# Every batch's attention in float32, with q, k and v laid out by the host: a fused attention and MoE kernel on one core

## The chip, the cores and the metric

The kernel runs on one core of one Trainium2 chip. The metric is the device time of one execution in microseconds (us); the number compared is the median of the timed runs. The engines are named as in the profile: PE (TensorE matmuls), PEld (TensorE weight loads), DVE (VectorE), ACT (ScalarE), POOL (GpSimd) and SP (SyncE, which here only issues DMA transfers).

## The reference

Three stages follow each other. The attention part, cut to what matters, is this (4 batches, 8 heads, 576 positions, 64 numbers a head):

```python
q_d, k_d, v_d = mean of every 4 rows of q, k, v         # 144 rows
out_d = softmax(q_d @ k_d.T / 8) @ v_d                  # pooled attention
out_up = repeat each row of out_d 4 times               # 576 rows again
scores = where(|i - j| < 4, q @ k.T / 8, -1e9)          # a band of 7
x = out_up + softmax(scores) @ v
...
xn = x / rms(x) * rms_g                                 # MoE1, x is 2304 x 512
x = ((silu(xn @ w_gate) * (xn @ w_val)) @ w_out)
y = (s * relu(x @ w_in) ** 2 + b) @ w_out2              # MoE2
```

The weights of both MoE stages are float64 in memory.

## The kernel before, in words

**The matmuls of MoE1 and MoE2.** A weight is read as pairs of 32-bit words, made float32 by two ACT and two DVE instructions a piece (L662 to L668), and split into a high and a low float16 half. Each product is three float16 matmuls (high·high, high·low, low·high). MoE1 goes over 8 blocks of 288 tokens. In a block, `moe1_gv` makes 12 pairs of `pg` and `pvl` (12 matmuls each, L746), then ACT takes a tanh (L753), DVE makes `u` in two instructions (L754, and `mul` at L210), and ACT and POOL split it (L757, L758). `moe1_out` makes four `po` of 36 matmuls (L768). The accumulators `pg`, `pvl` and `po` share one ring of PSUM tiles, so a new `pg` waits until DVE has read an older one.

**Attention.** A unit is a pair of heads, with four units to a batch. The local band is done in 9 windows of 64 queries against 70 keys, in two groups of 5 and 4 windows (`JS`). The pooled part has 144 queries in 3 pieces.

- Batches 0 and 1 (`early_unit`) use float32 on TensorE. q and k come in rows of 64 numbers (`load_unit`, L255), and TensorE turns them, 12 transposes (L463) and 4 copies on ACT (L465) a unit. POOL adds up groups of four columns (L468, L469). Scores `sl` (L482) start with a matmul that adds the mask (L478), the pooled scores are `sd` (L500), probabilities are turned (`tpl` L492, `tpd` L517) and multiplied with v (`pvd` L384, `pl` L400).
- Batches 2 and 3 (`attn_unit`) use float16 halves: ACT takes sums of squares for a scale (`stats`), ACT and DVE split q and k (L546, L547), SP turns them by DMA (L550), DVE copies q into blocks (`q_b` L554, `qd_b` L569), TensorE pools (`pd` L562), DVE and ACT split the probabilities (L575, L576, L584, L585), SP turns these too (L578, L588), and POOL and ACT split v (L150 to L152, into `vh` and `vdh`).

**What sets the order.** Attention of batch 0 runs first, with the preparation of the first weights beside it. Then `main01` makes MoE1 blocks 0 and 1. At every yield of it (a tick; mostly 12 matmuls) the generators of the side work take a step each: batch 1 from its start, batch 2 from tick START2 = 54. Blocks 2 to 5 (`middle`) carry batch 3 from START3 on. A unit starts every UNIT_STEP = 14 ticks in batches 2 and 3 and every 4 in batch 1, and `lag(n)` lets n ticks pass. From tick ORDERED = 50 on PE runs in the order in which the code is written (`tc.manual_schedule`); elsewhere and on the other engines a scheduler orders by priority. MoE2 follows MoE1. `warm` (L429) puts matmuls of no result into batch 0 that keep TensorE busy.

Of the kernel before, what the change touches and what calls it, by code (L numbers as in the profile page):

```python
# [32 lines left out]
NJ = 9  # L33
# [3 lines left out]
FLOATS = 4  # L37
HALF0 = 20
HALF_STEP = 12
# [3 lines left out]
LAG_SS = 3  # L43
LAG_PD = 6
LAG_SD = 3
LAG_SL = 2
LAG_VH = 3
LAG_V = 6
LAG_OD = 2
# [14 lines left out]
PDPE = 2  # L64
DEP = False
AMPB = 3
MASKB = 1
# [5 lines left out]
OFF = 0  # L73
OFF1 = 0
# [15 lines left out]
def kernel(  # L90
    ctx: ExitStack,
    tc: tile.TileContext,
    q: bass.AP,
    k: bass.AP,
    v: bass.AP,
# [37 lines left out]
    accs = [cp.tile([128, 2], F32, name=f"accs{i}") for i in range(2)]  # L133
# [8 lines left out]
    QB = (dve, dve)  # L142
    DEM = pool if DEP else dve
# [35 lines left out]
    def setup():  # L179
# [43 lines left out]
    P_d = ap.tile([128, 12, 128], F16, name="P_d")  # L223
    P_l = ap.tile([128, 18, 128], F16, name="P_l")
    q_b = ap.tile([128, 18, 2, 64], F16, name="q_b")
    qd_b = ap.tile([128, 2, 3, 128], F16, name="qd_b")

    def early_set(places):
        return {k: t[:, o:o + n] if t is not None else ap.tile([128, 2 * n], F16, tag=k, name=k + "0").bitcast(F32)
                for (k, n), (t, o) in zip((("qkT", 1152), ("PlT", 1152), ("vh", 1152), ("PdT", 768)), places)}  # L230

    def flat(t, pat):
        return t.rearrange(pat).bitcast(F32)

    def second_set():

        return early_set([(flat(P_l, "p a b -> p (a b)"), 0), (flat(q_b, "p j h q -> p (j h q)"), 0),
                          (ap.tile([128, 24 * 128], F16, tag="qk", name="qk0").bitcast(F32), 0),
                          (flat(P_d, "p a b -> p (a b)"), 0)])
# [20 lines left out]

    def load_windows(b, hp, vw):
        h0 = 2 * hp
        sp.dma_start(out=vw[:, :, 0, :], in_=v[b, h0:h0 + 2, 0:WIN, :].rearrange("h p d -> p h d"))
        sp.dma_start(out=vw[:, :, 8, :], in_=v[b, h0:h0 + 2, S - WIN:S, :].rearrange("h p d -> p h d"))
        for h in range(2):
            base = v[b, h0 + h, 61:62, 0:1]
            sp.dma_start(out=vw[:, h, 1:8, :],
                         in_=bass.AP(tensor=base.tensor, offset=base.offset, ap=[[D, WIN], [64 * D, 7], [1, D]]))
# [8 lines left out]
    def stats(hp, qkf, vd, junk):  # L277

        acc = accs[hp % 2]
        act.activation(out=junk[:, :1536], in_=qkf.rearrange("p t c h d -> p (t c h d)"), func=AF.Square,  # L280
                       accum_out=acc[:GR, 0:1])
        act.activation(out=junk[:72, :1024], in_=vd.rearrange("p a r d -> p (a r d)"), func=AF.Square,
                       accum_out=acc[:72, 1:2])
        accb = ap.tile([128, 2], BF16, tag="accb", name="accb")
        pool.tensor_single_scalar(out=accb, in_=acc, scalar=TINY, op=ALU.add)
        vs = sum4(vd)
        yield from lag(LAG_SS)
        ss = pX.tile([128, 2], F32, tag="x", name="ss")
        pe.matmul(out=ss, lhsT=ones_b, rhs=accb, start=True, stop=True)
        sc, iv = pow2(ap, ss, 2, 13, "sq", 2)  # L290
        cs = ap.tile([128, 2], F32, tag="cs", name="cs", bufs=2)
        mul(cs[:, 0:1], iv[:, 0:1], 1.0 / 8, iv[:, 0:1])
        dve.tensor_single_scalar(out=cs[:, 1:2], in_=iv[:, 1:2], scalar=2.0 ** -14, op=ALU.mult)
        return vs, sc, cs

    def softmax_d(sd, scale, de=None):
        dm = ap.tile([128, 3], F32, tag="dm", name="dm", bufs=2)
        dz = ap.tile([128, 3], F32, tag="dz", name="dz", bufs=2)
        dve.tensor_reduce(out=dm, in_=sd, axis=AX.X, op=ALU.max)
        dve.tensor_scalar(out=dm, in0=dm, scalar1=scale, scalar2=-1.0, op0=ALU.mult, op1=ALU.mult)  # L300
        if de is None:
            de = ap.tile([128, 3, SD], F32, tag="de", name="de")
# [10 lines left out]
    def scores_d(qd, cs):  # L313
        sd = pX.tile([128, 3, SD], F32, tag="x", name="sd")
        for o in range(3):
            for n, (lq, lk) in enumerate(((0, 0), (0, 1), (1, 0))):
                pe.matmul(out=sd[:, o, :], lhsT=qd_b[:, lq, o], rhs=qd[:, lk, SD:2 * SD], start=n == 0, stop=n == 2)
        de, dz = softmax_d(sd, cs[:, 0:1])
        dve.tensor_scalar(out=dz, in0=dz, scalar1=1e-9, scalar2=2.0 ** -12, op0=ALU.add, op1=ALU.mult)
        dve.reciprocal(out=dz, in_=dz)  # L320
        return de, dz

    def scores_l(qT, kT, js, mask_pe):

        m = len(js)
        sl = pS.tile([128, 5, WIN], F32, tag="s", name="sl")
        if mask_pe:
            pe.matmul(out=sl[:, :m, :], lhsT=ident_b, rhs=mask[:, js[0]:js[0] + m, :], start=True, stop=False,
                      skip_group_check=True)
        for j in js:  # L330
            for i, (lq, lk) in enumerate(((0, 0), (0, 1), (1, 0))):
                pe.matmul(out=sl[:, j - js[0], :], lhsT=qT[lq][:, j].rearrange("p h q -> p (h q)"),
# [825 lines left out]
```

## Time and profile before

| | |
|---|---|
| three timed runs | 1058.77, 1060.12, 1063.67 us; median 1060.12 us |
| profiled execution, span | 1059.3 us |
| PE busy | 976.0 us (92%) |
| DVE, ACT, POOL busy | 595.9, 518.1, 326.1 us |
| DMA packets | 128111, of which 111376 under 512 B |

The span runs from the first to the last instruction of the profiled execution; the runs' median lies 0.8 us above it. An engine's busy time is the union of its instructions. What PE does not fill of the span is waiting; part of its busy time can be at a lower granted clock.

### The profile page before, as it was taken

To read this page: it belongs to the slowest core of one execution; us is meant where nothing else is said; L and a number is where in the kernel's file an instruction comes from. 1 tells how busy PE (TensorE), PEld (TensorE's weight loads), DVE (VectorE), ACT (ScalarE), POOL (GpSimd) and SP (SyncE) were. 2 spreads that over 40 slices of the span, in tenths; PEclk is the share of its full clock that TensorE was granted. 3 is DMA by queue.
4 is the path that set the end of the run, shared out by engine and by line. 5 is a ranking of instruction groups with operands and counts; after the bars stand their busy time and mean duration, and the time that the engine had idled before them with its cause. 6 is when DMAs were issued, how large, how long until landed. Compare 5 with 4: busy or idle time off the path is not lost.

```text
span 1059.3 us, 20473 instructions
## 1 busy us (share of the span) xinstructions
PE 976.0 (92%) x8197; PEld 661.2 (62%) x8198; DVE 595.9 (56%) x1271; ACT 518.1 (49%) x1182; POOL 326.1 (31%) x417
## 2 busy tenths in 40 slices
PE   7985989998879799878999998999999999999998
PEld 4763767876658578756786676754555545455553
DVE  4788976725786645768627867474432414133240
ACT  3876687745546436544537877662322404132140
POOL 7443763354355455445451216320000000000000
PEclk9986999999999899998999999999999999999999
DMA  9884244102444323454204424200000000000000
GB/s 186 228 235 142 75 134 127 37 12 58 95 89 84 68 36 73 86 100 86 38 2 140 144 76 143 97 1 20 11 11 20 1 31 1 20 11 11 20 1 30
DMA packets 128111, 73.59 MB, mean 69 GB/s; under 512 B 111376, under 2 KB 115984, under 8 KB 128016
## 3 DMA queue, kind: packets, MB, share of 16 engines
q1 hardware_dynamic: 128016, 72.29, 26.8%
q8 instruction: 64, 1.05, 0.4%
q14 instruction: 31, 0.25, 0.1%
HBM read 54.97 MB, written 4.72 MB: 56 GB/s over the span
## 4 chain that ended last, share of the span: by engine, by line
PE 41%; DMA 5%; DVE 4%; ACT 3%; issue 1%; POOL 0%; SPq 0%; POOLq 0%; DVEq 0%; ACTq 0%
PE y L1120 18%; PE ph L1100 17%; DMA stg<-in_moe_w_in_dram 2%; PE pvl L746 2%; DMA stg<-in_moe_w_out_dram 2%; PE pg L746 2%; PE po L768 1%; DVE W L668 1%; DVE stg L664 1%; ACT stg L663 1%; ACT W L662 1%; DMA qkT<-qk 0%; DVE W L148 0%; DMA vw<-in_v_dram 0%; ACT W L147 0%
## 5 line engine op out<-in xcount | busy, mean ns | idle before, releaser
L746 PEld LDWEIGHTS <-W 128*128 128x128 f16 x2304 | 225.8, 100 | 99.9 <-issue 39.0
L1100 PE MATMUL ph<-X,W 128*128 128x384 f16 x1152 | 196.6, 326 | 0.4 <-DVE s4o L711 0.3
L746 PE MATMUL pg<-X,W 128*128 128x288 f16 x1152 | 167.7, 294 | 22.0 <-DVE u L754 20.8
L746 PE MATMUL pvl<-X,W 128*128 128x288 f16 x1152 | 164.9, 291 | 9.6 <-DVE u L754 4.9
L1100 PEld LDWEIGHTS <-W 128*128 128x128 f16 x1152 | 112.6, 98 | 81.2 <-issue 1.2
L1120 PE MATMUL y<-W 128*128 128x512 f16 x648 | 151.6, 379 | 0.0
L768 PE MATMUL po<-g,W 128*128 128x288 f16 x1008 | 132.4, 290 | 5.1 <-DVE u L754 4.3
L768 PEld LDWEIGHTS <-W 128*128 128x128 f16 x1152 | 112.9, 100 | 37.2 <-issue 7.4
L1104 ACT ACTIVATE r<-ph 128x384 f32<-128x384 f32 x96 | 46.9, 489 | 175.8 <-PE ph L1100 126.3
L758 POOL TENSOR_TENSOR g<-u,g 128x288 f16<-128x288 f32 x84 | 72.9, 868 | 133.4 <-ACT g L757 132.9
L1120 PEld LDWEIGHTS <-W 128*128 128x128 f16 x648 | 63.4, 98 | 71.0
L210 DVE SCALAR_TENSOR_TENSOR r<-ph,r 128x384 f32<-128x384 f32 x96 | 53.5, 557 | 59.1 <-ACT r L1104 59.1
L1125 DVE SCALAR_TENSOR_TENSOR ys<-y,ccol,bcol 128x512 f32<-128x512 f32 x18 | 13.5, 751 | 121.4 <-PE y L1120 119.2
L757 ACT ACTIVATE g<-u 128x288 f16<-128x288 f32 x84 | 36.8, 438 | 62.8 <-DVE u L210 61.1
L1108 DVE TENSOR_TENSOR W<-r,W 128x384 f16<-128x384 f32 x72 | 40.1, 557 | 36.6 <-ACT W L1107 36.6
L754 DVE SCALAR_TENSOR_TENSOR u<-u,pvl 128x288 f32<-128x288 f32 x96 | 43.0, 448 | 28.7 <-PE pvl L746 20.7
L1107 ACT ACTIVATE W<-r 128x384 f16<-128x384 f32 x72 | 37.5, 521 | 40.0 <-DVE r L210 40.0
L664 DVE SCALAR_TENSOR_TENSOR stg<-stg 128x512 int32<-128x512 int32 (+1 forms) x53 | 36.6, 690 | 33.7 <-ACT stg L663 33.6
L753 ACT ACTIVATE u<-pg,tsc 128x288 f32<-128x288 f32 x96 | 46.7, 487 | 9.4 <-PE pg L746 9.2
L1120 PE MATMUL y<-W,r2b 128*128 128x512 f16 x216 | 50.1, 379 | 0.0
L662 ACT ACTIVATE W<-stg 128x512 f32<-128x512 f32 (+1 forms) x53 | 34.1, 646 | 24.0 <-DMA stg<-in_moe_w_in_dram 10.7
L210 DVE SCALAR_TENSOR_TENSOR u<-u,pg 128x288 f32<-128x288 f32 x96 | 43.1, 449 | 1.6
(266 smaller groups left out, 1410.7 us busy)
## 6 DMA issues: line engine op xcount, KB each, us to landing
stg<-in_moe_w_out_dram SPq DMA_DIRECT2D x25, 512.0 KB
stg<-in_moe_w_in_dram SPq DMA_DIRECT2D x16, 512.0 KB
out_dram<-ys SPq DMA_DIRECT2D x18, 256.0 KB
W<-in_moe_w_gate_dram SPq DMA_DIRECT2D x10, 384.0 KB
W<-in_moe_w_val_dram SPq DMA_DIRECT2D x10, 384.0 KB
qkf<-in_q_dram SPq DMA_DIRECT2D x26, 144.0 KB
qkf<-in_k_dram SPq DMA_DIRECT2D x26, 144.0 KB
vd<-in_v_dram SPq DMA_DIRECT2D x13, 288.0 KB
```

The source lines that it names most:

```text
L210: (eng or dve).scalar_tensor_tensor(out=o, in0=a, scalar=s, in1=b, op0=ALU.mult, op1=ALU.mult)
L662: act.activation(out=dst, in_=stg[:, :, 1].bitcast(F32), func=AF.Copy, scale=2.0 ** -112)
L664: ins = dve.scalar_tensor_tensor(out=stg[:, :, 0], in0=stg[:, :, 1], scalar=-2 ** 31, in1=stg[:, :, 0], op0=ALU.bitwise_and, op1=ALU.bitwi ...
L746: pe.matmul(out=acc, lhsT=Cgv.half(o, FP, lw)[:, f0 * 128:f0 * 128 + 128], rhs=X16[:, kc, 3 * blk:3 * blk + 3, lx, :], start=i == 0, stop= ...
L753: act.activation(out=u, in_=ps[0], func=AF.Tanh, scale=tsc[:, part:part + 1])
L754: dve.scalar_tensor_tensor(out=u, in0=u, scalar=1.0, in1=ps[1], op0=ALU.add, op1=ALU.mult)
L758: pool.tensor_tensor(out=lo, in0=u, in1=hi, op=ALU.subtract)
L768: pe.matmul(out=acc, lhsT=Co.half(fc * 512, 512, lw)[:, m * 128:(m + 1) * 128], rhs=g16(fc)[:, lx, :], start=i == 0, stop=i == 35)
L1100: pe.matmul(out=acc, lhsT=C2.half((p * KC + kc) * 512, 512, lw)[:, f0 * 128:f0 * 128 + 128], rhs=X16[:, kc, 4 * blk:4 * blk + 4, lx, :], s ...
L1104: act.activation(out=r, in_=acc, func=AF.Relu, scale=2.0 ** -23)
L1108: dve.tensor_tensor(out=dst[:, 1, :], in0=r, in1=dst[:, 0, :], op=ALU.subtract)
L1120: pe.matmul(out=y, lhsT=src[:, lx, tt * 128:(tt + 1) * 128], rhs=C3.half(fc * 512, 512, lw), start=i == 0, stop=i == 47)
```

## The change

The host now lays out three arrays: `qk`, head dimension first, with two heads' q and k side by side (128 rows of 1152 numbers for a unit); `vwin`, v in the 9 windows of 70 rows; and `vgrp`, v in the 72 row groups of 8 rows that the pooled part reads. A unit has three loads. `attn_unit`, `stats`, `scores_d`, `scores_l` and `split_v` are gone; one `unit` serves all batches, in float32, without transposes of q and k. In it the multiply of the pooled probabilities is on DVE, the multiplies of the local ones are on POOL as before, and probabilities are turned 4 and 1 to a PSUM tile in place of 3 and 2. After batch 0, two units at a time have buffers of their own. Values of batch 2 are held until `main01` has ended. New lags: 3 ticks from the loads to the first scores, 3 from the last softmax to the first turn, 2 before the values.

```diff
-LAG_SS = 3
-LAG_PD = 6
-LAG_SD = 3
-LAG_SL = 2
-LAG_VH = 3
-LAG_V = 6
-LAG_OD = 2
+LAG_IN = 3
+LAG_SD = 1
+LAG_T = 3
+LAG_TD = 1
+LAG_V = 2
+LAG_O = 2
...
-    def load_unit(b, hp, qkf, vd, vw):
-        h0 = 2 * hp
-        for t, src in enumerate((q, k)):
-            for h in range(2):
-                sp.dma_start(out=qkf[:, t, :, h, :], in_=src[b, h0 + h].rearrange("(c p) d -> p c d", p=GR))
-        sp.dma_start(out=vd.rearrange("p a r d -> p a (r d)"),
-                     in_=v[b, h0:h0 + 2].rearrange("h (t p r) d -> p (h t) (r d)", p=72, r=4))
-        if vw is not None:
-            load_windows(b, hp, vw)
+    def load_unit(b, hp, st, vd):
+        sp.dma_start(out=st["qkT"], in_=qk[b, hp])
+        sp.dma_start(out=vd.rearrange("p a r d -> p (a r d)"), in_=vgrp[b, hp])
+        sp.dma_start(out=st["vw"][:WIN], in_=vwin[b, hp])
...
-    def early_unit(b, hp, sq_sum):
+    def unit(b, hp, sq_sum):
+
+        far = b >= 1
         if b == 0:
-            qkf, vd, vw = staged[hp]
-            st = early[hp]
+            vd, st = staged[hp]
             qd = Xf[:, hp, S + 1152:S + 1440]
         else:
-            st = second_set() if hp % 2 else early_set([(None, 0)] * 4)
-            qkf = ap.tile([GR, 2, 6, 2, D], F32, tag="qkf", name="qkf")
+            st = own_set()
             vd = ap.tile([72, 4, 4, D], F32, tag="vd", name="vd")
...
-                for i in range(3):
-                    pe.transpose(out=tp[:, i, :], in_=qkf[:, t, 3 * g + i].rearrange("p h d -> p (h d)"),
-                                 identity=ident_f[:GR, :GR])
-                act.activation(out=qT[:, 3 * g:3 * g + 3, :], in_=tp, func=AF.Copy)
...
         sl = local(JS[0])
+        if b == 0:
+            yield
+        a0 = softmax_l(sl, JS[0], pool)
+        if far:
+            yield
+        sl1 = local(JS[1])
+        if far:
+            yield from lag(LAG_SD)
         sd = pX.tile([128, 3, SD], F32, tag="x", name="sd")
...
+        dve.tensor_tensor(out=de, in0=de, in1=dz.unsqueeze(2).to_broadcast([128, 3, SD]), op=ALU.mult)
+        a1 = p1.tile([128, TB], F32, tag="u", name="a1", bufs=3)[:, :280].rearrange("p (j k) -> p j k", j=4) if b == 0 else None
+        a1 = softmax_l(sl1, JS[1], dve if b == 0 and hp == NP - 1 else pool, a1)
...
+        yield from lag(LAG_T if far else 1)
+        turn(a0, JS[0])
+        yield from lag(LAG_TD if far else 1)
...
-    def attn_unit(b, hp, sq_sum):
-        mp = b <= MASKB
...
-        for t in range(2):
-            act.activation(out=qv[:, t, 0], in_=qkv[:, t], func=AF.Copy, scale=sc[:GR, 0:1])
-            dve.scalar_tensor_tensor(out=qv[:, t, 1], in0=qkv[:, t], scalar=sc[:GR, 0:1], in1=qv[:, t, 0],
-                                     op0=ALU.mult, op1=ALU.subtract)
-        qkT = ap.tile([128, 24, GR], F16, tag="qkT", name="qkT")
-        sp.dma_start_transpose(out=qkT, in_=qk.rearrange("p a b -> p (a b)"))
...
+        turn(a1, JS[1])
+        if far:
+            yield from lag(LAG_V)
+        od = values_d(vs, PdT, b)
+        yield from lag(LAG_O if far else 1)
+        while b == 2 and not ended:
+            yield
+        for hh in range(2):
+            values_l(b, hp, JS[hh], vw, PlT, od)
```

On SP, at the head of the program, these rows of the kernel before are the first unit's loads and the start of the second's with the first piece of a weight (`W_86` is the space of the weights, in which q, k and the row groups are staged; `vh_111` takes the windows of v).

```order
L255 DMA W_86<-in_q_dram 96x6x64 x2
L255 DMA W_86<-in_k_dram 96x6x64 x2
L256 DMA W_86<-in_v_dram 72x4x256
L263 DMA vh_111<-in_v_dram 70x2x64
L264 DMA vh_111<-in_v_dram 70x2x64
L267 DMA vh_111<-in_v_dram 70x7x64 x2
L255 DMA W_86<-in_q_dram 96x6x64
L659 DMA W_86<-in_moe_w_gate_dram 128x768
```

In the changed kernel the same place of SP's queue reads as follows (`X` and `gx` lend space to the second and third unit).

```order
L216 DMA qkT<-in_qk_dram 128x1152
L217 DMA W_82<-in_vgrp_dram 72x1024
L218 DMA vw<-in_vwin_dram 70x1152
L478 DMA W_82<-in_moe_w_gate_dram 128x768
L216 DMA X<-in_qk_dram 128x1152
L217 DMA W_82<-in_vgrp_dram 72x1024
L218 DMA X<-in_vwin_dram 70x1152
L216 DMA gx<-in_qk_dram 128x1152
```

Ten DMAs stood ahead of the first weight, nine of them the first unit's; now three do, and the bytes of a unit's loads are nearly the same (128 x 1152, 72 x 1024 and 70 x 1152 numbers of four bytes).

On DVE, in a batch 3 unit of the kernel before, these rows stand in the order in which they run; the last one belongs to a MoE1 block.

```order
L547 SCALAR_TENSOR_TENSOR qk<-qkf,sqs,qk 96x768 x2
L585 TENSOR_TENSOR P_l<-ch,P_l 128x5x70
L585 TENSOR_TENSOR P_l<-ch,P_l 128x4x70
L554 COPY q_b<-qkT 64x18x64 x2
L754 SCALAR_TENSOR_TENSOR u<-u,pvl 128x288
L210 SCALAR_TENSOR_TENSOR u<-u,pg 128x288
```

In the changed kernel a batch 3 unit has this on DVE, from the last part of its local softmax to the pooled one (`L573` and `L185` are the two instructions on `u`).

```order
L573 SCALAR_TENSOR_TENSOR u<-u,pvl 128x288
L265 TENSOR_REDUCE z<-ch 128x4
L185 SCALAR_TENSOR_TENSOR u<-u,pg 128x288
L230 TENSOR_REDUCE dm<-sd 128x3
L266 TENSOR_SCALAR z<-z 128x4
L231 TENSOR_SCALAR dm<-dm 128x3
L267 RECIPROCAL z<-z 128x4
L392 TENSOR_SCALAR dz<-dz 128x3
L393 RECIPROCAL dz<-dz 128x3
L394 TENSOR_TENSOR de<-de,dz 128x432
L573 SCALAR_TENSOR_TENSOR u<-u,pvl 128x288
```

The two splits and the copies of q that stood ahead of `u` are gone, as are all other rows of the split; the multiply of `de` is new there, and what stands ahead of a `u` is now softmax work that waits for scores and for ACT's exponentials.

## Rows read from the trace of the kernel before

**Rows 1.** The page's head and its first part: span, busy time by engine.
```profile
span 1059.3 us, 20473 instructions
...
PE 976.0 (92%) x8197; PEld 661.2 (62%) x8198; DVE 595.9 (56%) x1271; ACT 518.1 (49%) x1182; POOL 326.1 (31%) x417
```

**Rows 2.** Busy time by stretch: stretch, length, engines, granted clock, DMA share, GB/s.
```profile
0.00:94.00 94.00, 71.18 (x792) 50.99 (x793) 69.86 (x161) 59.13 (x155) 46.70 (x74) 0.87 0.82 203
94.00:250.00 156.00, 145.43 (x1413) 112.75 (x1412) 108.82 (x244) 103.05 (x254) 79.89 (x101) 0.94 0.30 84
...
250.00:538.00 288.00, 252.50 (x2924) 198.39 (x2925) 190.41 (x450) 146.63 (x346) 138.22 (x157) 0.96 0.36 71
...
555.00:680.00 125.00, 114.90 (x901) 87.85 (x900) 87.45 (x164) 92.68 (x198) 44.42 (x41) 1.00 0.38 127
680.00:1059.30 379.30, 375.03 (x2020) 197.42 (x2017) 135.51 (x246) 110.72 (x217) 8.74 (x28) 1.00 0.04 13
```

**Rows 3.** Timeline of PE, the first projection matmul of MoE1.
```profile
93.95 0.40 PE L746 MATMUL pg<-X,W 128*128 128x288 f16 x1 [1.09 <-ACT X L632]
```

**Rows 4.** Timeline of DVE at the start: start, duration, instruction, idle before it.
```profile
13.62 0.56 DVE L664 SCALAR_TENSOR_TENSOR W<-W 128x384 int32<-128x384 int32 x1 [8.35 <-ACT W L663]
...
16.90 0.52 DVE L357 TENSOR_REDUCE z<-sl 128x5 f32<-128x350 f32 x1 [1.30 <-PE sl L482]
```

**Rows 5.** DMA traffic of the first 50 us.
```profile
DMA packets 20638, 10.37 MB, mean 207 GB/s; under 512 B 17662, under 2 KB 19102, under 8 KB 20632
```

**Rows 6.** Busy time in one late stretch of the start, columns as in rows 2.
```profile
80.00:90.00 10.00, 2.86 (x24) 2.08 (x23) 10.00 (x25) 6.71 (x15) 3.81 (x5) 0.50 0.61 158
```

**Rows 7.** PE's waits from 250 to 538 us: total, times, longest.
```profile
PE pg L746 <- DVE u L754: 15.9, 10, 3.2
PE pl L400 <- DVE poi L206: 5.9, 1, 5.9
PE pvl L746 <- DVE u L754: 4.9, 1, 4.9
PE po L768 <- DVE u L754: 3.5, 1, 3.5
```

**Rows 8.** Timeline of DVE from 488 us on.
```profile
488.48 2.73 DVE L547 SCALAR_TENSOR_TENSOR qk<-qkf,sqs,qk 96x768 f16<-96x768 f32 x2
491.13 3.04 DVE L585 TENSOR_TENSOR P_l<-ch,P_l 128x350 f16<-128x350 f32 x2
496.14 0.92 DVE L554 COPY q_b<-qkT 64x1152 f16<-64x1152 f16 x2 [1.97 <-DMA qkT<-qk]
```

**Rows 9.** Timelines of POOL and of PE at the same place.
```profile
490.36 3.51 POOL L152 TENSOR_TENSOR vh<-vw,vh 70x1152 f16<-70x1152 f32 x1
...
497.60 3.04 PE L746 MATMUL pvl<-X,W 128*128 128x288 f16 x12 [4.86 <-DVE u L754]
```

**Rows 10.** Timeline of PE: one accumulator's 12 matmuls, in batch 1's stretch.
```profile
203.23 1.63 PE L746 MATMUL pg<-X,W 128*128 128x288 f16 x12
204.70 0.29 PE L746 MATMUL pvl<-X,W 128*128 128x288 f16 x1
```

**Rows 11.** Groups of DVE from 238 to 538 us: busy, mean ns, idle before.
```profile
L547 DVE SCALAR_TENSOR_TENSOR qk<-qkf,sqs,qk 96x768 f16<-96x768 f32 x16 | 22.1, 1412 | 0.7 <-ACT qk L546 0.7
...
L585 DVE TENSOR_TENSOR P_l<-ch,P_l 128x280 f16<-128x280 f32 x8 | 10.1, 1258 | 2.2 <-ACT P_l L584 2.2
```

**Rows 12.** Line L746 alone over one float32 and one float16 unit: length, PE, PEld, clock.
```profile
164.25:190.63 26.38, 19.61 (x150) 14.07 (x148) 1.00 0.37 101
279.84:295.76 15.92, 12.79 (x99) 9.01 (x98) 1.00 0.54 107
```

**Rows 13.** All work from 164.25 to 190.63 us, columns as in rows 2; PE's transposes in it.
```profile
164.25:190.63 26.38, 26.38 (x290) 21.34 (x288) 16.19 (x43) 16.64 (x44) 11.27 (x15) 1.00 0.37 101
...
L463 PE MATMUL tp<-ident_f,qkf 96*128 96x96 f32 x12 | 1.5, 245 | 0.0
```

**Rows 14.** Timeline of PE: six pooled-score matmuls in float32 (12 records).
```profile
183.84 0.95 PE L500 MATMUL sd<-X 64*64 64x144 f32 x12
```

More of the change, by code (lines that the diff above doesn't have):

```diff
@@ L221, with own_set, lent_set @@
     ap = attn_cm.__enter__()
[L223 to L239, printed above, removed]
+    SET = (("qkT", 1152), ("PlT", 1152), ("vw", 1152), ("PdT", 768))
+    def own_set():
+        return {k: ap.tile([128, n], F32, tag=k, name=k, bufs=2) for k, n in SET}
+    def lent_set(places):
+        return {k: t[:, o:o + n] for (k, n), (t, o) in zip(SET, places)}
     gx = p1.tile([128, 3456], F32, tag="g16", name="gx")
@@ L275, in sum4 @@
         return vs
[L277 to L294, printed above, removed]
     def softmax_d(sd, scale, de=None):
@@ L301, in softmax_d @@
         if de is None:
-            de = ap.tile([128, 3, SD], F32, tag="de", name="de")
+            de = ap.tile([128, 3, SD], F32, tag="de", name="de", bufs=2)
         for o in range(3):
@@ L311, in lag @@
             yield
[L313 to L332, printed above, removed]
-                          rhs=kT[lk][:, win0(j):win0(j) + WIN], start=i == 0 and not mask_pe, stop=i == 2,
-                          skip_group_check=True)
-        return sl
     last = []
     normed = set()
+    ended = []
     gates = {}
@@ L346, in queued, with softmax_l @@
             yield
-    def softmax_l(sl, js, scale, zs, mask_pe, eng, a=None):
+    def softmax_l(sl, js, eng, a=None):
         m = len(js)
@@ L487, in turn @@
         def turn(a, js):
-            for j0 in range(js[0], js[0] + len(js), 3):
-                m = min(3, js[-1] + 1 - j0)
-                tp = turned(b, 128, "tpl")
+            for j0 in range(js[0], js[0] + len(js), 4):
+                m = min(4, js[-1] + 1 - j0)
+                tp = turned(b, m, "tpl")
                 for i in range(m):
@@ L518, in early_unit @@
             act.activation(out=PdT[:72, 3 * g:3 * g + 3, :], in_=tp[:72], func=AF.Copy)
-        a = p1.tile([128, TB], F32, tag="u", name="a1", bufs=3)[:, :280].rearrange("p (j k) -> p j k", j=4) if b == 0 else None
-        a = softmax_l(sl, JS[1], 1.0 / 8, 1.0, 1, dve if b == 0 and hp == NP - 1 else pool, a)
-        if b == 0 and hp % 2:
-            gates[1 + hp // 2] = tuple(last)
         yield
-        od = values_d(vs.unsqueeze(1), PdT, 0.25, ((0, 0),), b)
-        turn(a, JS[1])
-        yield
@@ L826, in attn_batch @@
         while gens or live:
-            if gens and n >= starts[NP - len(gens)]:
-                if b and NP - len(gens) == floats:
-                    clear()
+            if gens and n >= step * (NP - len(gens)):
                 live.append(gens.pop(0))
@@ L841, in attn_batch @@
         yield from later_norm(b, 1, sq_sum) if b else norm(b, 1, sq_sum)
-    def attn_later(b):
-        sq_sum = ap.tile([128, S], F32, tag="sqsum", name="sqsum")
-        if b == EARLY and FLOATS == NP:
-            clear()
-        gens = [attn_unit(b, hp, sq_sum) for hp in range(NP)]
-        live = []
-        n = halves_ = 0
-        while gens or live:
-            if gens and n % UNIT_STEP == 0:
-                live.append(gens.pop(0))
-            for g in list(live):
-                got = next(g, 0)
-                if got == 0:
-                    live.remove(g)
-                elif got == "half":
-                    halves_ += 1
-                    if halves_ == NP:
-                        live.append(later_norm(b, 0, sq_sum))
-            n += 1
-            yield
-        yield from later_norm(b, 1, sq_sum)
     def later_norm(b, hh, sq_sum):
@@ L1143 @@
     arrays, args = {}, []
-    for name in _INS:
-        a = _np.ascontiguousarray(inputs[name])
+    laid = dict(inputs)
+    heads = (B, NP, 2, S, D)
+    turned = [_np.asarray(inputs[n]).reshape(heads).transpose(0, 1, 2, 4, 3).reshape(B, NP, 128, S) for n in "qk"]
+    laid["qk"] = _np.concatenate(turned, axis=3)
+    v = _np.asarray(inputs["v"]).reshape(heads)
+    rows = _np.array([[win0(j) + i for i in range(WIN)] for j in range(NJ)])
+    laid["vwin"] = v[:, :, :, rows].transpose(0, 1, 4, 2, 3, 5).reshape(B, NP, WIN, 2 * NJ * D)
+    laid["vgrp"] = v.reshape(B, NP, 2, 2, 72, 4, D).transpose(0, 1, 4, 2, 3, 5, 6).reshape(B, NP, 72, 16 * D)
+    for name in ["qk", "vwin", "vgrp"] + _INS:
+        a = _np.ascontiguousarray(laid[name])
         if a.dtype == _np.float64:
```

232 lines of the change are left out of this document (51 added, 181 removed).

## The prediction

> **What bounds the kernel now.** I read the page's head first: PE is busy 976.0 of 1059.3 us [rows 1], so little can be won beyond PE's 83 us of waiting, apart from work that PE sheds. The busy time by stretch [rows 2] says where the waiting lies. From 680 us on PE works 375.0 of 379.3 us in MoE2, which the change does not touch. The rest falls on four stretches: the start, up to the first projection matmul at 93.95 us [rows 3], with 22.8 us without PE; batch 1's stretch (94 to 250 us) with 10.6; batches 2 and 3 (250 to 538 us) with 35.5; and 555 to 680 us with 10.1.
>
> In the start PE is no limit. Its work is attention and filler, and VectorE is busy 69.9 of 94 us, all of 80 to 90 us [rows 2, 6]. VectorE comes to its first softmax only at 16.90 us [rows 4].
>
> From 250 to 538 us the waits of PE name one thing: 24.3 us in 12 waits of `pg`, `pvl` and `po` are for `u` on DVE, and one of 5.9 us is for a small DVE step of a MoE1 block [rows 7]. Why `u` is late is seen at 488 us: VectorE splits q and k (2.73 us for two), then probabilities (3.04 us for two), then waits 1.97 us for the q that a DMA turns, and copies it; `u` stands behind all four [rows 8]. GpSimd splits v for 3.51 us in the same time. PE waits 4.86 us, and its next 12 matmuls take 3.04 us as the row counts them [rows 9], against 1.63 undisturbed [rows 10]: after the wait the clock is granted at the lower of its two levels, 1.2 GHz, for a while.
>
> **The change part by part.** The sum is made against the profiled execution, 1059.3 us of span, and 0.8 us is added for the runs' median, 1060.1.
>
> *Start, -8 us.* A unit's three loads hold 1.2 MB as its nine did, but 17662 of the first 50 us' 20638 packets were under 512 B, at 207 GB/s [rows 5]. The first scores now need only `qk`, 0.59 MB. At that same rate this saves 0.6 MB, 3 us. The first unit's 12 transposes go as well, 1.5 us of PE [rows 13], and their four copies with the waits in between; estimate another 3 us. So the first softmax begins about 6 us earlier. Behind it VectorE has 69.9 less 3 us of work in 77 us, some 10 us of gaps; earlier loads of the other units close a fifth of them, 2 us. VectorE's own work stays (weights are converted as before, softmax is the same), which is why I don't take more. Bounds: 3 us (the bytes alone) and 15 (nearly every gap closed).
>
> *Batch 1, -4 us.* Four units lose their transposes, 1.5 us each [rows 13]: 6 us of PE if PE is the limit throughout, which at 145.4 of 156 us it nearly is. Bounds 2 and 6; I take 4, since some of it falls into waits.
>
> *Batches 2 and 3, -15.5 us,* of four terms:
> - The waits, 35.5 us [rows 2], go if VectorE and GpSimd are relieved. VectorE loses two groups of 22.1 and 10.1 us [rows 11], the other half of the second split, the splits of the pooled probabilities, the copies of q and the scale's steps; it gains a multiply of `de` a unit, about as long as a softmax step of 0.5 us [rows 4]. GpSimd loses the 3.5 us split of v and more, and gains the sums of q and k. What stood ahead of `u` in one piece, 8.7 us at 488 us [rows 8], becomes softmax steps of some 0.5 us each. I take all 35.5 back; what returns is the last term.
> - The lower clock: 0.96 granted over 288 us costs at most 0.04 x 288 = 11.5 us. Nothing is lost where the clock was low while PE waited anyway. Bounds 0 and 11.5; I take 7, nearer to the upper, since the matmuls behind the wait in [rows 9] did run slow.
> - Float32 costs PE more. In batch 1 one float32 unit spans 26.38 us, with PE never idle [rows 13]; 150 of its matmuls are MoE1's [rows 12], at 0.1225 us each (1.47 us for 12, from start to start [rows 10]), 18.4 us. 8.0 are left to attention, 6.5 without the transposes. A float16 unit takes 15.92 - 99 x 0.1225 = 3.8 us [rows 12]. 2.7 us more for 8 units is +22 us. The upper bound counts the transposes as free: 4.2 x 8 = 34.
> - New waits, +5 us. PE's order is fixed, so it stops where scores wait for the `qk` load, issued 3 ticks (4.4 us) ahead, 2.8 us of which are bytes at 207 GB/s; and where a turn waits for softmax, VectorE and ScalarE by turns, and GpSimd's multiply. Behind a stopped turn stand the projections of MoE1, and behind those `u`. The nearest row is the float32 unit of batch 1, with no wait at all [rows 13]; the farthest is the 35.5 us of now. I take 5, near the first.
>
> *555 to 680 us, -3 us.* Batch 3 ends earlier, so its memory is free earlier, and conversions of MoE2's first weight move a block forward, ahead of the 10.1 us of waits here [rows 2]. Bounds 0 and 6.
>
> Sum: 1060.1 - 8 - 4 - 35.5 - 7 + 22 + 5 - 3 = 1029.6, so 1030 us.
>
> **The rivals.**
> - *The start gains nothing.* VectorE is its limit: in [rows 6] it never pauses, and if the earlier softmax only moves gaps behind, the first projection stays at 94 us. For it speaks that VectorE also converts weights there (from 13.62 us on [rows 4]), whose loads the change leaves alone; against it that 10 us of gaps lie after the first softmax. 1038 us, chance 0.10.
> - *Half of the waits stay.* `u` stays late, because softmax steps and `u` still share VectorE and come in bunches, with two units alive at a time. 0.5 x 42.5 = 21, in place of the 5 taken: 1046 us. Against it: a float32 unit in batch 1 leaves VectorE 10 of 26 us free [rows 13]. Chance 0.09.
> - *Float32 is dearer than batch 1 shows.* If the transposes filled holes that the scores would leave, each unit costs 8.0 us as before: +34 in place of +22, 1042 us. Chance 0.05. The Trainium skill has a rule of this direction (FP8 and Floating Point Precision, section TensorE Precision Notes): true float32 goes through the array in four passes. By it the six pooled-score matmuls, 144 columns each, would take 6 x 144 x 4 columns, 1.44 us at 2.4 GHz as an estimate; this case's trace disagrees, 0.95 us in two records each [rows 14]. By the rule a unit would be near 8.5 us (estimate) and the time about 1045 us.
> - *Slower: the turns stop PE.* The turn of the first windows follows the scores by about five accumulators, 7.4 us [rows 10]. Where a softmax chain is longer than that, because its steps queue behind `u` on VectorE or behind the split of g on GpSimd, PE stops once per unit, the projections start late, and the clock falls as in [rows 9]. At the size of today's waits and clock loss (42.5 us) this gives 1067 us. It decides from 5.1 us a unit on (41 us over 8 units lifts 1024.6 to 1065.4). Against it speaks [rows 13], where the same chain under the same projections makes no wait. Chance 0.05.
>
> **How the numbers follow.** The forecast, with gains in all four places, has 0.71; the rivals have 0.10, 0.09, 0.05 and 0.05. 1030 is its time, not a mean. If the better bounds of the start (15) and of the clock (11.5) come together with no new wait, 1013; I leave 0.08 below that. Above 1047 lie the last rival and the upper part of the second, 0.1. Range 1013 to 1047. A measurement of this kernel tells about 0.5%, 5.3 us, from no change: faster is below 1054.8, which every case but the last gives unless two join, 0.91; same 0.05; slower (above 1065.4) 0.04.
>
> **What would show it right or wrong.** In the changed kernel's profile the first softmax on DVE should stand near 11 us and the first `pg` near 86 us. PE's waits for `u` in the stretch of batches 2 and 3 should fall to a few us, and the granted clock there rise towards 1.00. One float32 unit should take PE 6.5 us beside the projections. From the first matmul of MoE2 on nothing should change. The forecast is wrong if new rows stand among PE's waits: `sl` for a `qk` load, `tpl` or `tpd` for POOL's multiply or DVE's `de`, each over 2 us and once a unit; or if `pg` stays at 94 us with VectorE full from 11 us on.

## The result, and the profile after

The changed kernel runs in 1036.88 us (median; 1034.98 to 1037.72) against 1061.11 us for the kernel before on the same chip. The ratio is 0.9771, with a 95% interval of 0.9751 to 0.9791. The profiled executions are 1034.3 and 1059.3 us long, 25.0 us apart; single executions differ from medians by a few us, so totals below are ratios and stretches are profile times.

The page's head of the changed kernel answers to [rows 1]: VectorE, ScalarE and GpSimd lost 85, 57 and 53 us of work, PE only 3.7.

```profile
span 1034.3 us, 19239 instructions
...
PE 972.3 (94%) x7862; PEld 658.5 (64%) x7870; DVE 510.5 (49%) x1095; ACT 461.6 (45%) x1070; POOL 272.9 (26%) x383
```

Cut at four events that PE's timeline of either kernel shows, the 25 us lie as follows (us; block 2 is the first behind `main01`, with batch 1's tokens; block 6 is the first behind all attention):

| from, to | before | changed | difference | forecast |
|---|---|---|---|---|
| start, first `pg` | 93.95 | 93.31 | -0.6 | -8 |
| first `pg`, `pg` of block 2 | 171.87 | 171.00 | -0.9 | -4 |
| `pg` of block 2, of block 6 | 290.02 | 264.43 | -25.6 | -15.5 |
| `pg` of block 6, first `ph` of MoE2 | 123.86 | 125.93 | +2.1 | -3 |
| MoE2 | 379.6 | 379.6 | 0 | 0 |

So the total came out near the forecast, 1030, with three of its four terms missed and one exceeded. That is luck in part: the start and the last stretch fell short by 12.5 us, the two in the middle made up 7 of them, and the first rival's 1038 lies nearer. The two middle terms were forecast for stretches that part at 250 us and not at block 2, so they are best taken together: -19.5 forecast, -26.5 measured. Busy time from block 2 to 6 in the kernel before (columns as in [rows 2]) is this:

```profile
265.82:555.84 290.02, 257.17 (x2949) 202.62 (x2948) 188.10 (x441) 143.37 (x337) 140.07 (x167) 0.96 0.35 69
```

And in the changed kernel, the start, that stretch, and the blocks ahead of MoE2:

```profile
0.00:94.00 94.00, 64.16 (x708) 44.58 (x714) 71.30 (x164) 51.63 (x131) 45.13 (x69) 0.79 0.71 209
...
264.31:528.74 264.43, 264.27 (x2677) 210.04 (x2677) 106.67 (x278) 112.78 (x285) 93.46 (x139) 1.00 0.12 36
...
530.00:655.00 125.00, 112.68 (x882) 87.00 (x882) 80.79 (x152) 83.56 (x182) 39.57 (x40) 0.97 0.34 102
```

PE's idle time from block 2 to 6 fell from 32.9 to 0.2 us, and the granted clock reads 1.00, its upper level. PE's busy time grew by 7.1 us all the same, since float32 costs more.

In the start, VectorE began softmax 4.9 us earlier than in [rows 4], and the first projection did not follow. VectorE's timeline shows the first softmax step and the end of the start (`L483` converts a weight, `L131` splits one, the `L295` at 85.18 is the last attention step of batch 0, `L430` the norm's first step):

```profile
11.57 0.56 DVE L483 SCALAR_TENSOR_TENSOR W<-W 128x384 int32<-128x384 int32 x1 [6.47 <-ACT W L482]
12.05 0.52 DVE L262 TENSOR_REDUCE z<-sl 128x5 f32<-128x350 f32 x1
...
79.63 5.63 DVE L131 SCALAR_TENSOR_TENSOR W<-W,rs 128x384 f16<-128x384 f32 x6
85.18 0.41 DVE L295 TENSOR_TENSOR X<-pl,od 128x256 f32<-128x256 f32 x1
85.52 3.25 DVE L131 SCALAR_TENSOR_TENSOR W<-W,rs 128x384 f16<-128x384 f32 x5
88.69 0.14 DVE L430 TENSOR_SCALAR ms<-ssn 96x3 f32<-96x3 f32 x1
```

PE's timeline has the first scores, the wait for what comes of the norm, and the row that answers to [rows 3]:

```profile
7.65 1.37 PE L360 MATMUL sl<-qkT 64*64 64x70 f32 x20
...
90.43 0.26 PE L442 MATMUL rb<-ident_b,rp 96*128 96x96 bf16 x1 [5.35 <-POOL rp L435]
...
93.31 0.40 PE L565 MATMUL pg<-X,W 128*128 128x288 f16 x1 [1.09 <-ACT X L451]
```

The timeline puts the 5.35 us on GpSimd, but GpSimd works from `ms`, and `ms` at 88.69 us stood behind five splits on VectorE, and these behind six more.

### The profile page after: what moved, and what is told of

Read it like the earlier page. It is cut to its first block, busy times and chain, and to the rows that moved or that the text cites. A ratio compares the mean times of both kernels' runs of the same rounds, so it can differ in the third digit from the quotient of the medians.

```text
span 1034.3 us, 19239 instructions
## 1 busy us (share of the span) xinstructions
PE 972.3 (94%) x7862; PEld 658.5 (64%) x7870; DVE 510.5 (49%) x1095; ACT 461.6 (45%) x1070; POOL 272.9 (26%) x383
## 4 chain that ended last, share of the span: by engine, by line
PE 68%; DVE 11%; DMA 10%; ACT 6%; issue 3%; POOL 1%; SPq 0%; ACTq 0%; DVEq 0%
PE y L904 18%; PE ph L884 18%; PE po L587 10%; PE pvl L565 7%; PE pg L565 7%; DMA stg<-in_moe_w_in_dram 3%; DMA stg<-in_moe_w_out_dram 3%; DVE W L131 2%; DMA W<-in_moe_w_val_dram 2%; DVE W L487 2%; ACT stg L482 1%; ACT W L481 1%; DVE stg L483 1%; DMA stg<-in_moe_w_gate_dram 1%; PE pl L291 1%
## 5 line engine op out<-in xcount | busy, mean ns | idle before, releaser
L565 PE MATMUL pg<-X,W 128*128 128x288 f16 x1152 | 163.1, 289 | 7.3 <-DVE u L573 4.4
L577 POOL TENSOR_TENSOR g<-u,g 128x288 f16<-128x288 f32 x84 | 67.1, 798 | 165.1 <-ACT g L576 145.7
L185 DVE SCALAR_TENSOR_TENSOR r<-ph,r 128x384 f32<-128x384 f32 x96 | 53.5, 557 | 59.4 <-ACT r L888 59.4
L573 DVE SCALAR_TENSOR_TENSOR u<-u,pvl 128x288 f32<-128x288 f32 x96 | 43.1, 449 | 79.0 <-PE pvl L565 75.8
L483 DVE SCALAR_TENSOR_TENSOR stg<-stg 128x512 int32<-128x512 int32 (+1 forms) x53 | 40.1, 757 | 39.9 <-ACT stg L482 39.7
L185 DVE SCALAR_TENSOR_TENSOR u<-u,pg 128x288 f32<-128x288 f32 x96 | 43.2, 449 | 2.0
```

Source lines behind the costliest of these rows:

```text
L185: (eng or dve).scalar_tensor_tensor(out=o, in0=a, scalar=s, in1=b, op0=ALU.mult, op1=ALU.mult)
L483: ins = dve.scalar_tensor_tensor(out=stg[:, :, 0], in0=stg[:, :, 1], scalar=-2 ** 31, in1=stg[:, :, 0], op0=ALU.bitwise_and, op1=ALU.bitwi ...
L565: pe.matmul(out=acc, lhsT=Cgv.half(o, FP, lw)[:, f0 * 128:f0 * 128 + 128], rhs=X16[:, kc, 3 * blk:3 * blk + 3, lx, :], start=i == 0, stop= ...
L573: dve.scalar_tensor_tensor(out=u, in0=u, scalar=1.0, in1=ps[1], op0=ALU.add, op1=ALU.mult)
L577: pool.tensor_tensor(out=lo, in0=u, in1=hi, op=ALU.subtract)
```

## The experiments

Theory A, after the result: the end of the start is set by what VectorE has queued, conversions and splits; batches 2 and 3 gained because VectorE and GpSimd were relieved, and PE is their only bound now; the missing rest went into new waits at 231 and 533 us. The rivals stand with each run. Theories C and D came after the first run. Ratios are to the kernel before on the same chip, with 95% intervals; the changed kernel's is 0.9771, and 0.001 is about 1 us.

**1. The rows alone.** Three loads a unit as in the change, but in short rows:

```diff
-        sp.dma_start(out=st["qkT"], in_=qk[b, hp])
+        sp.dma_start(out=st["qkT"].rearrange("p (c x) -> p c x", c=18), in_=qk[b, hp].rearrange("c p x -> p c x"))
...
+    for n_, c_ in (("qk", 18), ("vwin", 18), ("vgrp", 4)):
+        w_ = laid[n_]
+        laid[n_] = w_.reshape(w_.shape[:3] + (c_, w_.shape[3] // c_)).transpose(0, 1, 3, 2, 4)
```

> The changed kernel, with the same three loads a unit, but laid out in memory so that q, k and the windows of v come in rows of 256 bytes and the row groups in rows of 1 KB. Theory A (the start is set by VectorE's conversions and splits, and no load ends last later on): within 3 us of the changed kernel's 1036.9, first projection matmul at 93 us plus or minus 1. Rival (large rows do pay, 3 us in the start and more where loads are awaited): 5 us or more slower, with PE waits for qkT in batches 1 to 3.

Measured: 0.9723 (0.9697 to 0.9750), 1028.02 us, some 5 us *faster* than the changed kernel, which neither theory had. The first `pg` is at 83.71 us. In PE's timeline:

```profile
83.71 0.40 PE L565 MATMUL pg<-X,W 128*128 128x288 f16 x1 [4.82 <-ACT X L451]
```

And in the DMA traffic of the first 50 us, where most packets are short again, as in [rows 5]:

```profile
DMA packets 24125, 10.87 MB, mean 217 GB/s; under 512 B 21328, under 2 KB 22768, under 8 KB 24118
```

This was no comparison of rows alone, as the order of VectorE's instructions tells: the scheduler had ordered the start anew. Counted in that order are the conversion instructions ahead of batch 0's first attention step (a sum into `X`), with the time of that step, and the conversions and splits ahead of its last one, with the runs to come:

| kernel | rows of q, k | ahead of the first step; its time | ahead of the last | first `pg` | ratio |
|---|---|---|---|---|---|
| before | 256 B | 6; 37.02 | 46, 7 | 93.95 | 1 |
| changed | 4.6 KB | 15; 41.12 | 48, 11 | 93.31 | 0.9771 |
| rows of 256 B | 256 B | 6; 33.91 | 33, 8 | 83.71 | 0.9723 |
| rows of 512 B (6) | 512 B | 15; 46.73 | 48, 11 | 99.99 | 0.9837 |
| one gate moved (4) | 4.6 KB | 15; 40.86 | 32, 3 | 88.25 | 0.9813 |
| two gates moved (4) | 4.6 KB | 15; 40.85 | 16, 8 | 88.88 | 0.9912 |

Of the 9.6 us that the kernel with rows of 256 bytes gains at the first `pg`, 7.2 are there at the first attention step.

**2. Turning put back,** in batches 0 and 1, then in 2 and 3:

```diff
+        if b < 2:
+            for g in range(4):
+                tq = turned(b, 3, "tq")
+                for i in range(3):
+                    pe.transpose(out=tq[:GR, i, :], in_=qkT[:, 288 * g + 96 * i:288 * g + 96 * i + 96], identity=ident_f)
+                act.activation(out=st["PdT"][:GR, :384], in_=tq[:GR].rearrange("p a b -> p (a b)"), func=AF.Copy)
```

> The changed kernel, with 12 transposes of q and k and 4 copies on ScalarE put back into each unit of batches 0 and 1 (their result is not used). Theory A (PE and ScalarE have room in the start, and batch 1's stretch is limited by VectorE as much as by PE): 0 to 4 us slower, first projection within 1 us of 93.3. Rival (taking the turning out was worth the 12 us that the prediction gave it, and another loss hid them): 8 to 12 us slower.

Measured: 0.9858 (0.9836 to 0.9880), 9 us slower than the changed kernel, so the rival's size. It does not lie where the prediction had it: the first `pg` is at 95.36, 2.1 us later, and the stretch from there to block 2 took 178.4 us in place of 171.0. VectorE's order in the start is another one here as well, so the 2.1 us are no measure of the turning.

> The changed kernel, with the same 12 transposes and 4 copies in each of the 8 units of batches 2 and 3. Theory A (PE is busy 274.4 of 274.5 us there, so work on PE counts in full): 1.25 to 1.5 us a unit, 10 to 12 us slower. Rival (the stretch has hidden room): under 3 us slower.

Measured: 0.9947 (0.9929 to 0.9966), 18.7 us slower, more than the 10 to 12 expected. The transposes put back are 128 wide, those of [rows 13] 96, so each costs more: PE's group from 264 to 510 us has six units' 72 transposes.

```profile
L356 PE MATMUL tq<-ident_f,qkT 128*96 128x128 f32 x72 | 11.2, 280 | 1.8 <-ACT PdT L357 1.8
```

The stretch from block 2 to 6 is 277.76 us, 13.3 longer, which is these 11.2 us and their waits. The other 24 transposes of batch 2 ran ahead of block 2, and made that stretch 3.6 us longer. Theory A holds in kind: PE's work there counts in full, and its waits come on top.

**3. Work put back on VectorE and GpSimd,** in batches 2 and 3, with no reader (VectorE's part was also run by itself):

```diff
+            for t in range(2):
+                dve.scalar_tensor_tensor(out=jk[:GR, :768], in0=qkT[:GR, :768], scalar=1.0, in1=jk[:GR, :768],
+                                         op0=ALU.mult, op1=ALU.subtract)
+            for t in range(2):
+                dve.tensor_copy(out=jk[64 * t:64 * t + 64, :], in_=jk[64 * t:64 * t + 64, :])
...
+                dve.tensor_tensor(out=jv, in0=a_, in1=jv, op=ALU.subtract)
...
+            pool.tensor_tensor(out=pj, in0=st["vw"][:WIN], in1=ones_f[:WIN, 0:1].to_broadcast([WIN, 1152]), op=ALU.mult)
+            pool.tensor_tensor(out=ph_, in0=pj, in1=ph_, op=ALU.subtract)
```

> The changed kernel, with work of the removed kinds and sizes put back on VectorE (two 96x768 splits, two copies of 64 rows, two 128x350 and 128x280 subtractions, three 128x144 splits a unit) and on GpSimd (a 70x1152 multiply and a 70x1152 subtraction), in batches 2 and 3, with no reader. Theory A (the 35 us of waits came from what VectorE and GpSimd had to do): waits of pg, pvl and po for u come back, 12 to 35 us slower. Rival (they came from the chain split, DMA transpose, copy, which is not put back): under 5 us slower, PE busy over 98% of that stretch.

Measured: 1.0029 (1.0005 to 1.0054), 27 us slower.

> As the kernel with work put back on VectorE and GpSimd, but on VectorE alone. There the stretch from the first po to MoE2 was 15.6 us longer than in the changed kernel. Theory A1 (VectorE's load is what made u late): 10 to 15 us longer here too. Theory A2 (only the two together, GpSimd's reads standing in VectorE's way): 0 to 5 us.

Measured: 0.9840 (0.9814 to 0.9866), 7 us slower. In both kernels the start is longer as well, with VectorE in another order there (first `pg` at 98.55 and 100.21 us), so only the stretch from block 2 to 6 is compared. With both:

```profile
280.75:558.86 278.11, 268.60 (x2677) 211.54 (x2677) 150.63 (x338) 113.29 (x287) 120.70 (x151) 0.98 0.11 34
```

And with VectorE's part alone:

```profile
273.78:538.21 264.43, 264.27 (x2676) 209.85 (x2676) 137.65 (x338) 113.42 (x287) 93.57 (x139) 1.00 0.12 36
```

VectorE alone took 31 us more work without a cost: 264.43 us, to the hundredth the changed kernel's. With GpSimd's 27 us beside it the stretch is 13.7 us longer. From the first `pg` to block 2 it is 182.2 us with both and 173.6 with VectorE's alone. A1 falls. A2 wanted the two together, and GpSimd's part alone was not run, so GpSimd alone stays a rival to it. Theory A had expected waits for `u`; with both, PE's waits are others, and 5.1 of the 9.5 us in which it is idle are for `rp`, a step in GpSimd's own queue:

```profile
PE rb L465 <- POOL rp L458: 5.1, 3, 4.6
PE tpd L425 <- DVE de L405: 2.2, 1, 2.2
PE tpd L425 <- ACT PlT L382: 2.1, 1, 2.1
```

**4. Fewer conversions ahead, by gates.** The third quarter of the weights is held until batch 0's norm, then the second too:

```diff
-                with queued(min(p_, 3)) if p_ else nullcontext():
+                with queued((0, 1, 3, 3, 3)[p_]) if p_ else nullcontext():
```

(`(0, 3, 3, 3, 3)` in the second.)

> The changed kernel with its large rows, and one gate moved: the conversions of the third quarter of the gate and value weights are issued after batch 0's norm and not after its last softmax. On VectorE 32 conversion instructions and 3 splits then stand ahead of the last attention step of batch 0, where 48 and 11 stood. Theory C (what VectorE does ahead of that step sets when the projections begin; rows and transposes do not): 16 instructions of 0.55 us and some splits fewer, first projection 6 to 10 us earlier, 3 to 8 us faster than the changed kernel in all, since the weights are still needed. Rival D (small rows were faster because of how they share the DMA engines): first projection within 2 us of 93.3, no gain.

Measured: 0.9813 (0.9793 to 0.9834), 4 us slower, though the first `pg` came 5.1 us earlier.

> As the last, with the second quarter's conversions behind batch 0's norm too: 16 conversion instructions and 8 splits ahead of the last attention step. Theory C: first projection some 20 us earlier than in the changed kernel, but the second quarter is then awaited: total between 10 us faster and 5 us slower. Rival D: first projection within 2 us of 93.3.

Measured: 0.9912 (0.9890 to 0.9934), 15 us slower; the first `pg` came 4.4 us earlier, not 20. What the start gained was lost by the first `po`, which is at 212.8 and 218.1 us, against 209.4 in the changed kernel. Busy time from 60 to 75 us, with one gate moved:

```profile
60.00:75.00 15.00, 13.07 (x186) 10.24 (x184) 7.61 (x25) 5.36 (x13) 2.38 (x3) 0.82 0.16 65
```

VectorE works half of that time, where the changed kernel's VectorE is busy 13.79 of 15. A conversion that is held leaves a hole here, and the first `po` comes later.

**5. Batch 2 four ticks later.**

```diff
-START2 = 54
+START2 = 58
```

> The changed kernel with batch 2 begun at tick 58 in place of 54, so that its first pooled scores no longer come right behind the norm of batch 1, whose reader holds their only PSUM tile. Theory A (the 4.3 us wait of sd is that tile, and its clock loss): wait gone, 4 to 6 us faster than the changed kernel. Rival (the wait moves to the next matmul that needs the tile or to the end of batch 2): within 2 us.

Measured: 0.9732 (0.9707 to 0.9757), 4 us faster than the changed kernel; the two intervals touch, but the profiles show the gain where it was expected, with 430.1 us in place of 435.4 from the first `pg` to block 6. The longest wait of the changed kernel between 94 and 238.5 us was this (total, times, longest):

```profile
PE sd L386 <- DVE xn L448: 4.3, 1, 4.3
```

Its timeline shows the pooled scores slow behind it, 1.70 us against 0.95 in [rows 14]:

```profile
235.91 1.70 PE L386 MATMUL sd<-qd 64*64 64x144 f32 x12 [4.29 <-DVE xn L448]
```

With batch 2 begun later it is gone. Between 205 and 300 us the longest wait left is 0.9 us in two pieces:

```profile
PE sn L601 <- ACT x L593: 0.9, 2, 0.4
```

**6. Rows of 512 bytes,** (9, 9, 4) pieces in place of (18, 18, 4) in experiment 1, with every engine in the changed kernel's order.

> The changed kernel with q, k and the windows of v in rows of 512 bytes, the row groups in rows of 1 KB. Every engine's instructions stand in the changed kernel's order; in the kernel with rows of 256 bytes the scheduler had put softmax ahead of weight conversions on VectorE. Theory C (that order, and not the rows, made the start of the 256 byte kernel 9.6 us shorter): first projection within 2 us of 93.3, time within 3 us of the changed kernel, 0.9771 of the kernel before. Rival D (smaller rows share the DMA engines better): first projection at 84 to 90 us, 3 us or more faster.

Measured: 0.9837 (0.9821 to 0.9853), 7 us slower than the changed kernel. The first `pg` is 6.7 us later, and VectorE waits longer for its conversions (0 to 60 us; 11.6 in 4 in the changed kernel):

```profile
DVE W L483 <- ACT W L482: 15.2, 3, 8.7
```

So both theories fall. Rows do matter, the other way than D had it. SP's timeline shows where the time goes: the third piece of a weight is issued at 10.54 us in the changed kernel (first line) and at 18.24 here (second), behind loads whose issue lasts longer.

```profile
10.54 0.35 SPq L478 DMA_DIRECT2D W<-in_moe_w_gate_dram  x1
```

```profile
18.24 1.52 SPq L478 DMA_DIRECT2D W<-in_moe_w_gate_dram  x1
```

That the 256 byte kernel owes its gain to its order is then what is left, and not shown by itself: long rows in that order were not run.

**7. The blocks ahead of MoE2.** ScalarE of the changed kernel at 533 us shows why PE waits 5.03 us there for `x`: the copy stands behind conversions of MoE2's first weight that wait for their transfers.

```profile
533.59 0.66 ACT L481 ACTIVATE W<-stg 128x512 f32<-128x512 f32 x1 [2.89 <-DMA stg<-in_moe_w_in_dram]
534.15 0.64 ACT L482 ACTIVATE stg<-stg 128x512 int32<-128x512 uint16 x1
536.35 0.66 ACT L481 ACTIVATE W<-stg 128x512 f32<-128x512 f32 x1 [1.57 <-DMA stg<-in_moe_w_in_dram]
536.92 0.39 ACT L592 ACTIVATE xt<-po 128x288 f32<-128x288 f32 x1
537.21 0.40 ACT L593 ACTIVATE x<-po 128x288 bf16<-128x288 f32 x1
```

Two edits, the reader later or the conversions later:

```diff
-            if n == 1:
+            if n == 4:
                 run_posts()
...
-                with tc.high_priority(offset=SIDE):
+                with tc.high_priority(offset=SIDE), tc.issue_after(x5):
                     next(side, None)
```

> The changed kernel with the sums of the last block's output taken four steps into blocks 6 and 7, not one. Theory A (the 5.0 us wait of sn at 533 us is for a copy on ScalarE that stands behind a weight conversion, which waits for its transfer; the conversions came forward with the change): wait gone, 4 to 6 us faster than the changed kernel. Rival (another matmul waits there instead): within 2 us.

Measured: 0.9789 (0.9770 to 0.9809), no gain. The wait moved: `pvl` now waits 4.1 us for the same copy, whose PSUM tile it needs.

> The changed kernel with the conversions of MoE2's first weight held until ScalarE has made the last copy of block 5's output, as late as they were in the kernel before. Theory A (the 5.0 us wait of sn came from conversions that moved ahead of that copy on ScalarE, in whose order the copy waits for their transfers): wait gone; 3 to 5 us faster, unless the held conversions are then awaited. Rival E (blocks 6 and 7 are bound by the conversions' sum, wherever they stand): within 2 us, with the wait moved to u or to the first matmul of MoE2.

Measured: 0.9777 (0.9758 to 0.9795), no gain, and the stretch is 125.2 us long (125.9 in the changed kernel). The sums of `x` wait 1.8 us now, and the weight's own statistics wait instead:

```profile
PE st L794 <- ACT wsq L793: 4.1, 7, 1.2
...
PE sn L602 <- ACT x L593: 1.8, 2, 1.3
```

Rival E holds for both edits: these blocks take some 125 us wherever the conversions stand.

**8. What the runs point to:** experiments 1 and 5 together.

> The kernel with rows of 256 bytes, whose scheduler order puts softmax ahead of weight conversions on VectorE, and batch 2 begun at tick 58 in place of 54. If the two causes are apart, as theory C and theory A have them (order on VectorE in the start; the pooled scores' PSUM tile behind batch 1's norm), their gains add: 1028.0 of 1057.0 and 4 us less, a ratio of 0.968 to the kernel before, first projection at 84 us, no wait of sd. If the first projections of blocks 2 on are limited by the weights, the second gain is lost: 0.972.

Measured: 0.9660 (0.9632 to 0.9687), 1024.16 us, faster than both kernels; against the changed one some 12 us. The first `pg` came at 86.39 us, not 84, and the wait of `sd` is gone. The two gains add, within the intervals.

## Why the prediction was right in the sum, and where it failed

**The start (-8, measured -0.6): the step failed that lets the first projection follow the first softmax.** The scores of the first windows were complete on PE at 9.02 us, where VectorE had waited for them until 16.90 [rows 4], so the loads and the turning gave more than the 6 us of the step. VectorE came to them at 12.05 us, right behind a conversion at 11.57 for which it had waited 6.47 us: it takes its queue in order, and ScalarE's part of that conversion had waited 8.54 us for the weight's transfer. At batch 0's first attention step the gain had become a loss. These are that step before (first line) and in the changed kernel (second):

```profile
37.02 0.49 DVE L405 SCALAR_TENSOR_TENSOR X<-pl,od 128x320 f32<-128x320 f32 x1
```

```profile
41.12 0.48 DVE L295 TENSOR_TENSOR X<-pl,od 128x320 f32<-128x320 f32 x1
```

The scheduler had put 15 conversion instructions ahead of that step, where 6 stood. At the step that the first norm needs, the last but one, the kernels are level (79.70 and 79.23 us); then `ms` follows 16 splits in place of 8, and runs 1.1 us later than before. The first rival had the time right (1038 us for a start that gains nothing) and half of the reason. VectorE was not full: it stood idle 11.6 us in the first 60, behind conversions whose weights were on their way. The short rows did cost something: with the order unchanged, rows of 512 bytes make the start 6.7 us longer. What the turning cost in the start stays open. The order with softmax first comes with 9.6 us more at the first `pg`. Whether long rows in that order would give more again was not tried: the scheduler changes the order with the rows. The gates, which leave the 15 conversions where they were, show that the number ahead of the last step is not what counts; that it is whether VectorE is kept at work is likely by the holes there, and not shown.

**Batch 1 (-4, measured -0.9): right in kind, but not all of the work lay there, and other work and a wait took its place.** With 128 wide transposes back in, the stretch grew by 7.4 us, so the turning was on the path there. The term took the transposes of four units; those of one ran in the start. Batch 2, on the other hand, reaches further into this stretch than before. These are groups of PE from the first `pg` to block 2, before:

```profile
L463 PE MATMUL tp<-ident_f,qkf 96*128 96x96 f32 x36 | 4.6, 248 | 0.4 <-ACT P_l L465 0.4
...
L317 PE MATMUL sd<-qd,qd_b 128*128 128x144 f16 x9 | 0.7, 226 | 0.0
```

And in the changed kernel:

```profile
L370 PE MATMUL tpl<-ident_f,ch 128*70 128x128 f32 x45 | 7.1, 274 | 3.1 <-ACT PlT L371 2.7 <-POOL vs L224 0.2 <-POOL W L135 0.2
L386 PE MATMUL sd<-qd 64*64 64x144 f32 x72 | 6.5, 317 | 4.3 <-DVE xn L448 4.3
```

A float32 unit has 9 records of `tpl` and 12 of `sd`, so beside batch 1's four units the scores of two and the turns of one unit of batch 2 run here now, where one float16 unit's scores did: some 5 us more, as an estimate from the starts in PE's timelines. The wait is at a place that the prediction's last term didn't look at, the seam to batch 2: the pooled scores share one PSUM tile with batch 1's norm, and PE's fixed order stops on them (4.3 us and the clock behind it). Moving batch 2's start removes it.

**Batches 2 and 3 (-15.5, measured -25.6): right in mechanism, with the clock mis-sized and the border in the way.** The waits went, 32.9 us to 0.2. New waits were 0 in this stretch, not 5; the 4.3 us of `sd`, ahead of it, belong to a unit of batch 2. Float32 cost a little more than 2.7 us a unit. From 402.09 to 430.07 us, one cycle of a unit:

```profile
402.09:430.07 27.98, 22.10 (x169) 15.94 (x168) 1.00 0.12 35
```

These are MoE1's matmuls alone; 14 ticks of 12 at 0.1225 us are 20.6, four of the sums take 0.5, and 6.9 us are left to attention, 3.1 more than a float16 unit. By the four-pass rule of the Trainium skill (FP8 and Floating Point Precision, section TensorE Precision Notes) the prediction had estimated 8.5 us a unit; the trace has less again. Whether the rule fails, or the matmuls of two heads, 64*64 in the rows, overlap in the array, no run here separates.

What the clock gave shows only in both stretches together, where it doesn't matter which unit lies on which side of the border. From the first `pg` to block 2, before and changed:

```profile
93.95:265.82 171.87, 158.65 (x1549) 123.06 (x1549) 114.98 (x261) 112.33 (x278) 87.01 (x109) 0.93 0.29 79
```

```profile
93.31:264.31 171.00, 155.66 (x1577) 118.91 (x1577) 116.22 (x258) 102.24 (x256) 86.17 (x108) 0.97 0.27 82
```

With the rows of block 2 to 6 above, the terms come out so (us; estimates are marked):

| term, both stretches | forecast | measured |
|---|---|---|
| PE's waits | -35.5 + 5 | -30.6 (46.1 to 15.5) |
| batch 1's transposes | -4 | -4.6 |
| float32 in batches 2 and 3 | +22 | +25 (estimate, 8 x 3.1) |
| clock | -7 | -16 (estimate, what is left) |
| sum | -19.5 | -26.5 |

So the waits came out as forecast, and the term that was mis-sized is the clock's: the prediction sought it from 250 to 538 us alone, but the granted clock rose by 0.04 in both stretches, which allows up to 18.5 us.

The reason given for the waits was too narrow. VectorE's load by itself costs nothing (264.43 us with 31 us of it put back). With GpSimd's beside it, the stretch is 13.7 us longer, and 9.5 of the 32.9 us of waits are back, none of them for `u`. GpSimd's part alone was not run, and neither was the chain of split, DMA transpose and copy; what made `u` late in the kernel before stays open between them.

**555 to 680 us (-3, measured +2.1): the sign was wrong.** The conversions did come forward (ScalarE begins them at 506.91 us, 22 us ahead of block 6, and began them at 555.93, with block 6), and ScalarE's queue put the last copies of a block behind them. Two ways of taking that wait away gave nothing, as other waits took its place; what bounds these blocks is not shown.

## What to carry to other kernels

A transfer that lands earlier gives time only if the in-order queue that uses it lets the work pass: count what stands ahead of the steps on its way, the first of them too, and look whether that queue waits for something else meanwhile. Where a scheduler orders the work, any change of a load's shape may reorder an engine that it does not touch; compare the orders before comparing times. A forecast by stretches should be cut at events that the change does not move work across, or be compared over stretches taken together. And a removed load on two engines should be put back on each of them alone before either, or both, is called the cause.

## What the runs showed of the hardware

VectorE's 128x350 subtraction with both inputs in SBUF lasts 519 ns in the kernel with VectorE's load alone and 808 ns with GpSimd's load beside it:

```profile
L413 DVE TENSOR_TENSOR jk<-ch,jk 128x350 f16<-128x350 f32 x8 | 4.1, 519 | 0.7 <-POOL ch L270 0.3
```

```profile
L415 DVE TENSOR_TENSOR jk<-ch,jk 128x350 f16<-128x350 f32 x8 | 6.5, 808 | 0.5 <-POOL ch L272 0.3
```

The Trainium skill (SBUF — State Buffer, section SBUF: two separate sides) says that such an instruction and a GpSimd one that reads SBUF lock each other out of a shared pair of ports; the trace agrees with its direction, 808 against 519 ns. The 128x280 subtractions of the same kernels did not change, 441 and 439 ns.

In the first 50 us the loads ran at 217 GB/s with rows of 256 bytes, 210 with 512 and 249 with 4.6 KB. The Trainium skill (DMA: Bandwidth & Descriptors, section Specifications) gives 512 bytes as the least size for full rate; these runs do not bear it out: with the order unchanged, rows of 512 bytes ran at 210 GB/s where rows of 4.6 KB ran at 249. All share their time with the weights' loads, so the rates are of the mixture.
